# Starting the fast stages of a retention + expert-mixture kernel earlier, on one Trainium2 core

## The chip, the cores and the metric

One core of one Trainium2 chip. The metric is device microseconds (us) of one execution. Every total time below is a median of several executions, all in the same, undisturbed state; times inside a kernel are from one traced execution. Each engine runs its own instruction stream. In this program TensorE makes the matrix products, VectorE, ScalarE and GpSimd the element-wise work, and SyncE issues most transfers. GpSimd issues transfers as well, on a queue of its own.

## The reference

```python
# q, k, v: 8 batches, 8 heads, 576 tokens, 64 wide, float32
scores = (q @ k.transpose) / sqrt(64)
ret = scores * Dmat                     # Dmat: gamma_h ** (i - j) for j <= i, else 0
attn = ret @ v
x = attn, heads side by side            # 4608 tokens x 512
p = domain_probs / domain_probs.sum(-1)
out = 0
for e in range(4):                      # w1[e]: 512 x 1024, w2[e]: 1024 x 512
    out += p[:, e] * (relu(x @ w1[e]) @ w2[e])
```

The products are made in bfloat16 with float32 sums.

## The kernel before

The 4608 tokens are nine **tiles** of 512. For each tile and each expert there are two **units** of TensorE work: an up unit (x @ w1) and a down unit (h @ w2). A unit exists in two forms. The **classical** form is 32 products of 512 columns. The **seven-product** form splits each matrix into 2 x 2 blocks and makes seven block products instead of eight: 56 products of 256 columns. It needs sums of blocks of the weights, tokens and hidden values, which VectorE makes first (`weight_sums`, `down_sums`, `token_sums`, `hidden_sum`). So a unit can be fast only when weights and tokens have come early enough for their sums.

The program has a **head**, all classical, and then **stages**. A stage (tile, expert) runs the up unit of its own expert and, in four **fills** between its products, the down unit of the stage before it. The order of all instructions is fixed when the program is built. The attention of the batches is spread between these products: batch 0 and 1 by a fixed plan in the head, batches 2 to 7 by a list (`Chain`) that gives out pieces once they can be ready. A batch has 512 tokens in chunks and a **remainder** of 64.

Loads of q, k and v come in two forms. Batch 0 is loaded in token pairs, so that a run in memory is 512 bytes; all others in pieces with runs of 256 bytes:

```python
def load_paired(b):
    raw_units(b)
    for x, (hf, u) in enumerate(UNITS):          # four units: two halves x two groups of heads
        h = slice(4 * u, 4 * u + 4)
        for n, src in SRC:
            nc.sync.dma_start(out=state[b][n, x].rearrange("p (h x) -> p h x", h=4),
                in_=src[b, h, 256 * hf:256 * hf + 256, :].rearrange("h (p j) d -> p h (j d)", j=2))

def load_piece(b, n, c):
    t = state[b][n, c]
    return nc.sync.dma_start(out=t.rearrange("p (h d) -> p h d", h=H),
                             in_=dict(SRC)[n][b, :, c * C:(c + 1) * C, :].rearrange("h p d -> p h d"))
```

The results of the four experts are added either on the chip (first and last tile) or by the transfer that writes them (all others):

```python
def on_chip(nt):
    return nt in (0, n_nt - 1)

def send(nt, e, pair, j):                       # two of them, 512 KB each, for one (tile, expert)
    x = slice(...)                              # cut
    if e == 0:
        i = nc.sync.dma_start(out=out_rows[:, x, :], in_=acc[nt, j])
    else:
        i = nc.gpsimd.dma_start(out=out_rows[:, x, :], in_=acc[nt, j], accum_op=ADD)
    ...
```

The order of the weight loads, the plan of the head, and the stages:

```python
load_w1(1, 0); load_w1(1, 1)
w20 = load_w2(0)
load_w2(1)
for e in range(2, E):
    load_w1(e)
    load_w2(e)
load_next(w20); load_next(); load_next()        # remainder of batch 0
raw_units(1)
for c in range(2):                              # batch 1, unpaired
    for n in "kqv":
        load_piece(1, n, c)
...
at(25, begin1)                                  # the rest of batch 1, and batch 1's casts
for c, g in enumerate((39, 41, 43, 45)):        # batch 1's four chunks
    at(g, lambda c=c: a1().T(c))
    ...
head += [up_classical(0, 1), down_groups(0, 0), down_groups(0, 1), up_classical(0, 2), down_groups(0, 2),
         up_classical(0, 3), down_groups(0, 3), up_classical(1, 0, lead=2, cut=3 * NT // 4)]
...
for nt, e in [(nt, e) for nt in range(1, n_nt) for e in range(E)][1:]:   # stages (1, 1), (1, 2), ...
    ...
```

So before, five up units (expert 0 to 3 of tile 0, expert 0 of tile 1) and their five down units are classical, and all others have seven products.

Of the kernel before, what the change touches and what calls it, by code (L numbers as in the profile page):

```python
# [9 lines left out]
FP32 = mybir.dt.float32  # L10
# [13 lines left out]
def kernel(  # L24
# [66 lines left out]

    def raw_units(b):

        state[b] = {}
        for x in range(4):
            t = wpool.tile([128, 3, H * D], FP32, tag=f"w2s_{x}", name="raw")
            for i, (n, _) in enumerate(SRC):
                state[b][n, x] = t[:, i]

    def load_paired(b):  # L100
        raw_units(b)
        for x, (hf, u) in enumerate(UNITS):
            h = slice(4 * u, 4 * u + 4)
            for n, src in SRC:
                nc.sync.dma_start(
                    out=state[b][n, x].rearrange("p (h x) -> p h x", h=4),
                    in_=src[b, h, 256 * hf:256 * hf + 256, :].rearrange("h (p j) d -> p h (j d)", j=2))
# [36 lines left out]
    def load_w1(e, part=None):  # L144
        if not part:
            w1_sb.append(wpool.tile([128, NDC, F], BF16, tag=f"w1_{e}", name="wt1"))
        f = slice(0, F) if part is None else slice(part * F // 2, (part + 1) * F // 2)
        return nc.gpsimd.dma_start(out=w1_sb[e][:, :, f], in_=moe_w1[e, :, f].rearrange("(dc p) f -> p dc f", p=128))
# [7 lines left out]
    load_paired(0)  # L156
# [249 lines left out]
    class AttP(Att):  # L406

        rem_states = (1, 3)

        def cast(self, n, hf, u, eng):  # L410
            if (n, u) == ("k", 0):
                self.half(hf)
            h = slice(4 * u, 4 * u + 4)
            if n != "v":
                self.m[n, hf, u] = att1.tile([128, 2, 4, D], BF16, tag=n + "m", name=n + "m", bufs=3)
            o = self.m[n, hf][:, :, h, :] if n == "v" else self.m[n, hf, u]
            i = self.t[n, 2 * hf + u].rearrange("p (h j d) -> p j h d", h=4, j=2)
            if n in gain:
                g = gain[n][:, NCH + 1 + 2 * hf:NCH + 3 + 2 * hf, h]
                eng.tensor_tensor(o, i, g.unsqueeze(3).to_broadcast([128, 2, 4, D]), op=MULT)  # L420
            else:
                eng.tensor_copy(o, i)
# [71 lines left out]


# [4 lines left out]
    def on_chip(nt):  # L500
        return nt in (0, n_nt - 1)

    def out_pair(nt, e, pair, j):

        if e == 0 or not on_chip(nt):
            acc[nt, j] = apool.tile([128, 2, Dm], FP32, tag="acc", name="acc")
        return acc[nt, j]

    def send(nt, e, pair, j):
        x = slice(nt * NSUB + pair[0], nt * NSUB + pair[1] + 1, pair[1] - pair[0])  # L510
        if e == 0:
            i = nc.sync.dma_start(out=out_rows[:, x, :], in_=acc[nt, j])
        else:
            i = nc.gpsimd.dma_start(out=out_rows[:, x, :], in_=acc[nt, j], accum_op=ADD)  # L514
            for p, d in sent[nt, e - 1]:
                if set(p) & set(pair):
                    after(i, d)
        sent.setdefault((nt, e), []).append((pair, i))
# [25 lines left out]
    def downs(nt, e, ring):  # L544

        hT = hTs[nt, e]
        def evacuate(po, ns):
            t, pair, j = nt * NSUB + ns, (ns // 2 * 2, ns // 2 * 2 + 1), ns // 2
            a = (acc[nt, j] if ns % 2 else out_pair(nt, e, pair, j))[:, ns % 2]
            pe = probs[:, e, t:t + 1]  # L550
            if e == 0 or not on_chip(nt):
                nc.scalar.activation(a, po, Copy, scale=pe)
            else:
                nc.vector.scalar_tensor_tensor(a, po, pe, a, op0=MULT, op1=ADD)
            if not on_chip(nt):
                if ns % 2:
                    send(nt, e, pair, j)
            elif e == E - 1:
                nc.sync.dma_start(out=out[t * 128:(t + 1) * 128, :], in_=a)

        for ns in range(NSUB):
            po = bank(ring, [128, Dm], FP32, "po")
            for fc in range(NFC):
                nc.tensor.matmul(po, lhsT=hT[:, fc, ns * 128:(ns + 1) * 128],  # L564
                                 rhs=w2_sb[e][:, fc, :], start=(fc == 0), stop=(fc == NFC - 1))
                yield None if fc < NFC - 1 else lambda: evacuate(po, ns)
# [58 lines left out]
    class Down:  # L625
# [37 lines left out]
        def out(self, i):  # L663
# [5 lines left out]
            if e and on_chip(nt):  # L669
# [5 lines left out]
            if i == 1 and not on_chip(nt):  # L675
                send(nt, e, pair, j)
# [51 lines left out]
    warm(8)  # L728
# [3 lines left out]
    for x, (hf, u) in enumerate(UNITS):  # L732
# [14 lines left out]
        a0.kv(hf, u)  # L747
    transposed_probs()
# [8 lines left out]
    for e in range(2, E):  # L757
        load_w1(e)
        load_w2(e)
# [4 lines left out]
    for c in range(2):  # L764
        for n in "kqv":
            load_piece(1, n, c)
# [12 lines left out]
    class Chain:  # L779
        def __init__(self):  # L780
# [5 lines left out]
            self.now, self.begun, self.tokens, self.late = 0, {(1, "r"): -1}, 2 * S - R, []  # L786
# [87 lines left out]
        def emit(self, kind, nt, strict=True):  # L874
# [4 lines left out]
            for k, n in need.items():  # L879
# [8 lines left out]
                elif k == "tile":  # L888
                    ok = n <= nt + 2
# [27 lines left out]
    def casts1(*cs):  # L917
        for c in cs:
            for n in "kqv":
                state["a1"].cast(n, c, nc.gpsimd)  # L920

    def begin1():
        state["a1"] = Att(1)
        casts1(0)
        for c in range(2, NCH):
            for n in "kqv":
                load_piece(1, n, c)
        casts1(1, 2)
        load_ahead(7)

# [4 lines left out]

    def rem1_casts():
        for n in "kqv":
            a1().cast_rem(n, nc.gpsimd)
            loads["cast"] += 1
            load_ahead(len(PIECES))  # L940
        a1().dmaT(NCH)

    def a1():
        return state["a1"]
# [3 lines left out]
    at(29, a0.Trem)  # L948
    at(31, a0.Srem, a0.Srem_mask)
    at(34, a0.Orem, lambda: a0.x(NCH, nc.vector))  # L950
    at(25, begin1)
    for c, g in enumerate((39, 41, 43, 45)):
        at(g, lambda c=c: a1().T(c))
        at(g + 1, lambda c=c: (a1().S(c), a1().kv_chain(c)))
        if c > 0:
            at(g + 1, lambda c=c: a1().O(c - 1))
        at(g + 1, lambda c=c: (a1().mask(c, 0), a1().mask(c, 1)))
        if c > 0:
            at(g + 1, lambda c=c: a1().x(c - 1, nc.vector))
    at(47, lambda: (a1().O(3), a1().x(3, nc.vector)))  # L960

    def narrow():
        RINGS["at"] = ("a0", "a1", "a2")
        turn.update(at=0)

    at(42, lambda: casts1(3))
    at(46, rem1_casts)
    at(48, narrow, lambda: state.update(t1=token_sums(1)), lambda: [state["t1"].pop(i)() for i in (0, 0, 1)])

    def sums_at(kind, e, *gs):  # L970
        todo = []
        for i, g in enumerate(gs):
            at(g, lambda i=i: (todo or todo.extend(kind(e)), todo[i]()))
        return todo

    sums_at(weight_sums, 1, 16, 17, 18, 19)
    s0 = sums_at(weight_sums, 0, 20, 21, 22)
    sums_at(weight_sums, 2, 26, 28, 30, 31)
    sums_at(down_sums, 1, 42, 43, 44, 48)
    sums_at(weight_sums, 3, 36, 38, 49, 50)  # L980
    s2 = sums_at(down_sums, 2, 51, 52, 53)
    at(50, lambda: a1().put_krem(nc.gpsimd, a1().qr[:, 1]))
    for g in range(48, 56):
        at(g, lambda: pool(1, 1))

    head += [up_classical(0, 1), down_groups(0, 0), down_groups(0, 1), up_classical(0, 2), down_groups(0, 2),
             up_classical(0, 3), down_groups(0, 3), up_classical(1, 0, lead=2, cut=3 * NT // 4)]
    g = 0
    for work in head:
        for _ in work:  # L990
# [3 lines left out]
            if g > 48:  # L994
                chain.now += 1


    turn.update(po=0)
    state["t1"].pop()()
    def stage(nt, e):  # L1000
        return nt * E + e

    begin = {1: (1, 1), 2: (1, 2), 3: (1, 3), 0: (2, 0)}
    owed = [((1, 1), (2, 0), s0[3]), ((1, 1), (1, 3), s2[3])]
    for e in (3, 0):

        use, last = stage(*begin[e]) + 1, stage(*begin[e]) - E + 2
        owed += [(divmod(last if i == 3 else 0, E), divmod(use, E), f) for i, f in enumerate(down_sums(e))]

    def pay(nt, e, late=False):  # L1010
        for x in owed:
            if x[1] <= (nt, e) if late else x[0] <= (nt, e):
# [5 lines left out]
    before, gaps = (1, 0), 0  # L1018
    for nt, e in [(nt, e) for nt in range(1, n_nt) for e in range(E)][1:]:
        fast = before >= begin[before[1]]  # L1020
# [8 lines left out]
        def between(i):  # L1029
# [3 lines left out]
            if i == 3:  # L1033
                pool(nt, 4 if gaps < 8 else 3 - g)
# [4 lines left out]
        def fill(i):  # L1039
            if i == 4:  # L1040
                chain.put_late()
            if not fast:
                for _ in range(4):
# [28 lines left out]
        def last_sum():  # L1072
            if g == 1 and (nt, e) >= begin[e]:
# [5 lines left out]
        def sums(i):  # L1079


            old, new = before in hsum, (nt, e) >= begin[e]
            turns = {(0, 1): 0 if old else 2, (0, 2): 0 if old else 1, (0, 3): 1,
                     (1, 1): 2, (1, 2): 1, (1, 3): 1}[g, i]
            while (e, g, i) == (0, 0, 2) and front:
# [4 lines left out]
            if g == 1 and new:  # L1090
# [120 lines left out]
```

## Time and profile before

| | before |
|---|---|
| median of 3 executions | 515.34 us (515.08 to 516.17) |
| span in the trace | 514.5 us |
| TensorE busy | 98% |
| read from / written to memory | 45.16 MB / 31.46 MB |
| stage (1, 2), the first stage that both kernels run at the same place with the same past work | starts at 105.31 us |

The prediction below shows most of the views. Two more are needed for the comparison. The chain of work that ended last, as shares of the span, says who set the end:

```profile
PE 92%; DVE 5%; issue 1%; DMA 1%; ACT 0%; SPq 0%; DVEq 0%; ACTq 0%
```

The windows view gives the busy time of TensorE, weight load, VectorE, ScalarE and GpSimd (number of instructions in brackets), the granted clock, the share of DMA (1.00 is 16 engines full, and it may pass that where transfers overlap) and GB/s. The stretch in question:

```profile
40.00:85.00 45.00, 44.63 (x339) 22.62 (x343) 29.27 (x48) 15.98 (x30) 19.93 (x22) 1.00 1.06 197
```

TensorE works 44.63 of 45 us. The transfers are just as full, at a share of 1.06, and TensorE hardly feels it: what it asks for is nearly always there.

### The profile page before, as it was taken

How to read it: one execution, taken by the hardware profiler on the slowest of the kernel's cores; microseconds unless marked ns; L12 is line 12 of the kernel's file. 1: busy time of each engine (PE TensorE's matmuls, PEld its weight loads, DVE VectorE, ACT ScalarE, POOL GpSimd, SP SyncE). 2: the span in 40 equal slices, each digit the busy share in tenths (PEclk: the TensorE clock that was granted, in tenths of full speed). 3: DMA queues.
4: the chain of work that ended last, by engine and by line, in shares of the span. 5: the costliest groups of instructions: out<-in, count | busy, mean ns of one | idle time of the engine just before them, and what ended most of it. 6: DMA issues, size and time to landing. Idle time of an engine off the chain costs nothing.

```text
span 514.5 us, 12795 instructions
## 1 busy us (share of the span) xinstructions
PE 504.1 (98%) x4923; PEld 405.7 (79%) x4934; DVE 374.4 (73%) x696; ACT 336.0 (65%) x693; POOL 251.1 (49%) x345
## 2 busy tenths in 40 slices
PE   8999999999999999999999999999999999999995
PEld 3644455688888888888888888888888888888884
DVE  5724479878777777768777877886778777667785
ACT  3462263677667766777767776777777767777663
POOL 6702275756644656466645664476457521321012
PEclk9999999999999999999999999999999999999998
DMA  9999997959797799969997999789987652565002
GB/s 239 187 207 201 208 196 184 165 146 186 120 172 194 115 177 161 182 142 183 133 223 140 162 153 212 159 144 154 173 195 122 94 83 83 83 86 80 1 2 82
DMA packets 160749, 76.27 MB, mean 148 GB/s; under 512 B 131724, under 2 KB 144524, under 8 KB 160688
## 3 DMA queue, kind: packets, MB, share of 16 engines
q1 hardware_dynamic: 141648, 44.79, 44.8%
q0 software_dynamic: 18752, 30.41, 38.2%
q8 instruction: 38, 0.62, 0.5%
q10 hardware_dynamic: 288, 0.26, 0.2%
q14 instruction: 23, 0.19, 0.1%
HBM read 45.16 MB, written 31.46 MB: 149 GB/s over the span
## 4 chain that ended last, share of the span: by engine, by line
PE 92%; DVE 5%; issue 1%; DMA 1%; ACT 0%; SPq 0%; DVEq 0%; ACTq 0%
PE upP L691 21%; PE downV L645 20%; PE downW L645 15%; PE upR L691 10%; PE ph L525 7%; PE po L564 6%; PE upQ L691 5%; PE s L328 2%; PE oc L379 1%; PE kvp L346 1%; PE oc L376 1%; DMA raw<-in_q_dram 1%; PE warm_out L164 1%; DVE qm L420 1%; DVE sT L333 0%
## 5 line engine op out<-in xcount | busy, mean ns | idle before, releaser
L691 PEld LDWEIGHTS <-wt 128*128 128x128 bf16 x992 | 94.9, 98 | 14.5 <-issue 1.4
L645 PEld LDWEIGHTS <-hT 128*128 128x128 bf16 x960 | 93.7, 98 | 12.0
L716 POOL TENSOR_SCALAR hT<-hT 128x512 bf16<-128x512 bf16 x62 | 38.1, 614 | 108.9 <-DVE hT L715 108.7
L645 PE MATMUL downV<-wt,hT 128*128 128x256 bf16 x480 | 81.8, 272 | 0.0
L691 PEld LDWEIGHTS <-wsum 128*128 128x128 bf16 x744 | 72.6, 98 | 9.1 <-issue 0.2
L707 DVE TENSOR_TENSOR upR<-upP,m 128x512 f32<-128x512 f32 x62 | 43.3, 699 | 48.6 <-ACT downW L651 39.9
L645 PEld LDWEIGHTS <-hsum 128*128 128x128 bf16 x720 | 70.0, 98 | 8.8 <-DVE hsum L617 0.3
L691 PE MATMUL upP<-xT,wt 128*128 128x256 bf16 x496 | 74.4, 272 | 0.7 <-DVE xT L595 0.5
L723 ACT ACTIVATE hT<-upP 128x512 bf16<-128x512 f32 x62 | 37.0, 597 | 52.0 <-PE upP L691 36.8
L514 POOL DMA_DIRECT2D out_dram<-acc x42 | 51.3, 1221 | 30.7 <-ACT acc L672 23.9
L674 DVE TENSOR_SCALAR acc<-downV,probs 128x512 f32<-128x512 f32 x56 | 42.0, 749 | 30.1 <-PE downV L645 29.7
L718 ACT ACTIVATE hT<-upR 128x512 bf16<-128x512 f32 x62 | 37.0, 597 | 31.3 <-PE upR L691 31.3
L709 ACT ACTIVATE hT<-upQ 128x512 bf16<-128x512 f32 x62 | 37.0, 597 | 15.9 <-PE upQ L691 15.9
L715 DVE TENSOR_TENSOR hT<-upP,m 128x512 bf16<-128x512 f32 x62 | 42.8, 690 | 5.8 <-PE upP L691 4.4
L672 ACT ACTIVATE acc<-downW,probs 128x512 f32<-128x512 f32 x56 | 38.6, 690 | 9.2 <-PE downW L645 9.2
L340 POOL TENSOR_SCALAR_AFFINE_SELECT sT<-sT 128x512 bf16<-128x512 bf16 x24 | 15.4, 643 | 57.4 <-ACT sT L339 48.0
L541 ACT ACTIVATE hT<-ph 128x512 bf16<-128x512 f32 x40 | 23.5, 597 | 29.8 <-PE ph L525 28.9
L697 ACT ACTIVATE upQ<-upP 128x512 f32<-128x512 f32 x62 | 37.0, 597 | 2.5 <-PE upP L691 2.3
L691 PE MATMUL upP<-tsum,wt 128*128 128x256 bf16 x248 | 37.2, 273 | 0.0
L691 PE MATMUL upR<-tsum,wsum 128*128 128x256 bf16 x248 | 37.2, 273 | 0.1
L691 PE MATMUL upP<-tsum,wsum 128*128 128x256 bf16 x248 | 37.2, 273 | 0.0
L691 PE MATMUL upR<-xT,wsum 128*128 128x256 bf16 x248 | 37.2, 273 | 0.0
(149 smaller groups left out, 1032.9 us busy)
## 6 DMA issues: line engine op xcount, KB each, us to landing
out_dram<-acc POOLq DMA_DIRECT2D x42, 512.0 KB, 6.5
out_dram<-acc SPq DMA_DIRECT2D x14, 512.0 KB, 4.1
wt<-in_moe_w_dram POOLq DMA_DIRECT2D x6, 1024.0 KB, 25.2
raw_k<-in_k_dram SPq DMA_DIRECT2D x24, 256.0 KB, 4.4
raw_q<-in_q_dram SPq DMA_DIRECT2D x24, 256.0 KB, 3.5
raw_v<-in_v_dram SPq DMA_DIRECT2D x24, 256.0 KB, 4.2
raw<-in_k_dram SPq DMA_DIRECT2D x8, 256.0 KB, 5.6
raw<-in_q_dram SPq DMA_DIRECT2D x8, 256.0 KB, 5.6
```

Source lines behind the costliest of these rows:

```text
L514: i = nc.gpsimd.dma_start(out=out_rows[:, x, :], in_=acc[nt, j], accum_op=ADD)
L645: nc.tensor.matmul(o, lhsT=l[:, k, self.s * 128:(self.s + 1) * 128], rhs=r[:, k], start=(i == 1 and k == 0), stop=(k == NFC // 2 - 1), ski ...
L672: nc.scalar.activation(a, po, Copy, scale=pe)
L674: nc.vector.tensor_scalar_mul(a, po, pe)
L691: nc.tensor.matmul(ps[:, l], lhsT=wa(kc)[:, f:f + 128], rhs=xa(kc), start=(start and l == 0 and kc == 0), stop=(kc == 1), skip_group_check ...
L697: nc.scalar.activation(Q, P, Copy)
L707: nc.vector.tensor_tensor(R_, P, m5, op=ADD)
L709: nc.scalar.activation(hT[:, lo, t0], Q, Relu)
L715: nc.vector.tensor_tensor(h22, P, m5, op=ADD)
L716: nc.gpsimd.tensor_scalar(h22, h22, float("inf"), 0.0, op0=MIN, op1=MAX)
L718: nc.scalar.activation(hT[:, lo, t1], R_, Relu)
L723: nc.scalar.activation(hT[:, hi, t0], P, Relu)
```

## The change

The intent is to leave the classical form sooner. Tile 1 begins right after expert 2's up unit of tile 0, and tile 0's expert 3 comes later, as a stage between (1, 1) and (1, 2). Batch 1 must then be ready some 20 us sooner, so it is loaded in token pairs, as batch 0 was, before the second half of the weights. And as tile 0 isn't finished before tile 1 begins, only experts 0 and 1 of tile 0 are added on the chip: that result is written at once, and experts 2 and 3 are written as adding transfers. The core of the diff (the class for paired attention of batch 1, `AttQ`, is cut to its head, as are the lists of sums):

```diff
+    class AttQ(AttP):                     # batch 1 in four token-pair units
+        rem_states = (0, 1, 2, 3)         # states not summed: later units use 2 or 10 more products
+        ...
-    def on_chip(nt):
-        return nt in (0, n_nt - 1)
+    def adds(nt, e):
+        return e > 0 and (nt == n_nt - 1 or (nt, e) == (0, 1))
+    def sends(nt, e):
+        return nt < n_nt - 1 and (nt, e) != (0, 0)
@@ send
-        if e == 0:
+        if (nt, e - 1) not in sent:
             i = nc.sync.dma_start(out=out_rows[:, x, :], in_=acc[nt, j])
@@ start
-    warm(8)
+    warm(10)
         a0.kv(hf, u)
+        if x < 3:
+            warm(2)
@@ loads
-    for e in range(2, E):
-        load_w1(e)
-        load_w2(e)
+    w12 = load_w1(2, 1)
+    load_w1(2, 0)
...
-    for c in range(2):
-        for n in "kqv":
-            load_piece(1, n, c)
+    ORDER1 = (0, 2, 1, 3)
+    for x in ORDER1:
+        load_unit(1, x, w12)              # held until the first half of w1 of expert 2 is in
@@ plan of the head
+    at(3, lambda: cast1(0, "kv"), lambda: cast1(1, "kv"), lambda: load_w2(2), lambda: cast1(2, "kv"))
+    at(21, a0.Trem)                       # remainder of batch 0
+    at(22, a0.Srem, lambda: cast1(0, "q"), a0.Srem_mask)
+    at(23, lambda: a1.T(*UNITS[0]))       # batch 1
+    at(24, a0.Orem, lambda: a0.x(NCH, nc.scalar))
+    ...
+    at(25, lambda: cast1(3, "kv"), lambda: load_w1(3, 0), lambda: load_w1(3, 1), lambda: load_w2(3))
+    at(29, lambda: load_ahead(6))         # remainder of batch 1
...
-    head += [up_classical(0, 1), down_groups(0, 0), down_groups(0, 1), up_classical(0, 2), down_groups(0, 2),
-             up_classical(0, 3), down_groups(0, 3), up_classical(1, 0, lead=2, cut=3 * NT // 4)]
+    head += [up_classical(0, 1), down_groups(0, 0), down_groups(0, 1), up_classical(0, 2)]
@@ stages
+    stages = [(1, 0), (1, 1), (0, 3)] + [(nt, e) for nt in range(1, n_nt) for e in range(E)][2:]
...
-                for _ in range(4):
+                for n in range((8, 2, 2, 4)[i - 1] if g == 0 else 4):
+                    if (g, i, n) == (0, 1, 4):
+                        visit1(4, 3)      # batch 1's last values, inside the first fill
+                        t1.pop(0)()
+                        front.extend(t1)
                     f = next(fill_classical)
```

## The prediction

> **What bounds the kernel now.** I read the page's busy shares and its forty slices first, then the list of what TensorE waited for, then TensorE's timeline from 20 to 125 us, then the table of engines by windows, then the DMA view.
>
> ```profile
> PE 504.1 (98%) x4923; PEld 405.7 (79%) x4934; DVE 374.4 (73%) x696; ACT 336.0 (65%) x693; POOL 251.1 (49%) x345
> ...
> PE   8999999999999999999999999999999999999995
> ...
> DMA  9999997959797799969997999789987652565002
> GB/s 239 187 207 201 208 196 184 165 146 186 120 172 194 115 177 161 182 142 183 133 223 140 162 153 212 159 144 154 173 195 122 94 83 83 83 86 80 1 2 82
> ```
>
> TensorE is full in every slice but the first and the last. Waits give the reader the same thing from the other side; the columns are microseconds in all, times, longest:
>
> ```profile
> PE pt L429 <- DVE qm L420: 1.4, 3, 0.8
> PE warm_out L164 <- DVE kbd L159: 1.3, 1, 1.3
> PE o L481 <- DVE sT L469: 0.7, 2, 0.4
> PE upP L691 <- DVE xT L595: 0.5, 2, 0.3
> PE upP L691 <- DVE upR L707: 0.2, 1, 0.2
> ```
>
> Five entries, 4.1 us in all, and 3.4 us of that before 20 us. So the kernel is bound by the amount of TensorE work. A change gains what it takes out of TensorE's own stream, and loses any new wait that it puts there; moving work between the other engines gains nothing by itself.
>
> The sizes come from TensorE's timeline (start, duration, then what ran):
>
> ```profile
> 18.46 0.42 PE L463 MATMUL s<-qkT 64*64 64x128 bf16 x16
> 18.81 0.72 PE L447 MATMUL kvp<-vm,km 64*128 64x128 bf16 x8
> 34.71 13.98 PE L564 MATMUL po<-wt,hT 128*128 128x512 bf16 x63
> 48.52 5.34 PE L525 MATMUL ph<-xT,wt 128*128 128x512 bf16 x24
> ...
> 66.70 0.39 PE L309 MATMUL ptc<-ident,qm 128*128 128x128 bf16 x4
> 111.43 0.60 PE L691 MATMUL upP<-xT,wt 128*128 128x256 bf16 x4
> 111.86 0.60 PE L691 MATMUL upR<-tsum,wsum 128*128 128x256 bf16 x4
> 112.30 0.60 PE L645 MATMUL downV<-wt,hT 128*128 128x256 bf16 x4
> ```
>
> Starts, not durations, give the cost, as ends overlap. Two classical down units of 32 products of 512 columns run from 34.71 to 48.52 us: 13.81 us for 64, so 0.2158 us each and **6.91 us a unit** (one record of the 64 is missing). In the fast stages four products of 256 columns take 111.86 - 111.43 = 0.4375 us on average, 0.1094 each. A unit in seven products is 7 x 2 x 2 x 2 = 56 of them: **6.13 us**.
>
> **What the Trainium skill says.** "TensorE: Matmul & The Clock Gate", section "Wait — 56ns, not 53.3ns?": a warm stream advances by N/2.4 GHz plus about 2.5 ns, 215.7 ns at 512 columns. The trace agrees: 215.8, and 109.4 against a worked-out 109.2 at 256. The same section gives a floor of about 25 ns between starts of small products; here sixteen 64x64 products of 128 columns take 18.81 - 18.46 = 0.35 us, 22 ns each, so the measurement is a little lower, and I use 22 ns. "DMA: Bandwidth & Descriptors", section "Queues, rings and completion order": each DMA engine goes round its queues packet by packet. The trace agrees, in the DMA view of 36 to 38 us (packets, MB, share):
>
> ```profile
> q0 software_dynamic: 181, 0.37, 96.3%
> q1 hardware_dynamic: 179, 0.05, 17.3%
> ```
>
> Equal packets, but 2 KB each for weights and about 256 B each for the unpaired loads of q, k, v. Its section "Specifications" asks for 512 B at least per transfer for line rate. The trace agrees again, in the windows table (last column GB/s; 5 to 10 us is batch 0 in token pairs, 35 to 40 weights beside unpaired loads, 65 to 70 unpaired loads alone):
>
> ```profile
> 5.00:10.00 5.00, 4.30 (x32) 1.91 (x33) 2.72 (x5) 0.66 (x2) 2.36 (x4) 1.00 1.14 295
> 35.00:40.00 5.00, 5.00 (x25) 2.28 (x24) 0.17 (x1) 1.88 (x3) 0.00 (x0) 1.00 1.14 206
> 65.00:70.00 5.00, 4.95 (x49) 2.77 (x49) 2.98 (x5) 3.86 (x8) 3.68 (x4) 1.00 0.97 191
> 75.00:80.00 5.00, 4.94 (x51) 2.73 (x51) 5.00 (x8) 1.35 (x3) 4.01 (x6) 1.00 0.67 130
> ```
>
> **The change part by part.**
>
> *Four units in seven products.* Before, five up units (expert 0 to 3 of tile 0, expert 0 of tile 1) and their five down units are classical. After, only experts 0 to 2 of tile 0 are. Two ups and two downs change: 4 x (6.91 - 6.13) = **3.1 us off** TensorE, all of it on the path.
>
> *Batch 1 in token pairs.* Before, its four chunks of transposes, scores, states and values sit between 66.70 and 83.49 us. Adding the start-to-start pieces of the timeline (0.44 + 0.58 + 0.45 + 0.80 + 0.44 + 1.03 + 0.66 + 1.04 + 0.58) gives 6.0 us. After, there are four units. Each has eight transposes, 0.44 us; sixteen small state products, sixteen score and sixteen value products, about 0.35 us each; and 128-column products with all earlier states, since states are no longer summed: 2 in a first-half unit, 10 in a second-half one, at 0.055 us. That is 4 x 1.49 + 24 x 0.055 = 7.3 us, so **1.3 us on**. The remainder of batch 1 now takes four states instead of one: 12 more products of 64 columns at about 0.029 us (four start 0.11 us apart from the next group), **0.35 us on**.
>
> *Warm-up products.* Two more at the start, where TensorE waits 0.85 us for the first q anyway, and two after each of three head units (0.43 us each). In that stretch VectorE is busy 4.2 to 4.5 of 5 us and TensorE waits for its casts and masks. They fill waits: nothing to 0.1 us.
>
> *Output of tile 0.* Experts 2 and 3 go out as adding transfers: four more issues on GpSimd (1.22 us each, with GpSimd at 49%) and 2.1 MB more of DMA. Off the path, but it moves data into a crowded time, below.
>
> Sum of TensorE work: -3.1 + 1.3 + 0.35 + 0.1 = **-1.4 us**. The order of stages itself, and the 8, 2, 2, 4 split of classical fill, move work and add none. What the split does: the last values of batch 1 run inside the first fill, and 4 classical products plus one group (0.86 + 0.44 us) lie between them and the product that needs their token sum. ScalarE must copy three pieces (about 0.9 us) and VectorE subtract (0.42 us), some 1.5 us with the handing over. I add **0.2 us** of wait.
>
> **Where new waits can come from: the load order.** Before, weights land one after the other: w1 of expert 1 at 26.4, w2 of 0 at 31.3, w2 of 1 at 36.6, w1 of 2 at 42.4, w2 of 2 at 49.0, w1 of 3 at 54.8, w2 of 3 at 61.5 us (issue plus time to landing). After, batch 1 starts when the first half of w1 of expert 2 is in, near 40 us. Paired units landed 2.7 us apart for batch 0. So, with half a weight (0.5 MB) beside them, I expect unit 0 near 46 us, unit 1 near 49, unit 2 near 52; then w2 of expert 2 starts and takes two bytes for one, and w2 and unit 3 are in near 59 and 60 us. TensorE asks for them, adding the pieces above from 48.5 us on: unit 0 at 49, unit 1 at 52, unit 2 at 55.5, unit 3's k and q (cast) at 59 and v at 61, w2 of expert 2 at 63.5. Two to three microseconds of slack at first, about none for unit 3: I book **0.3 us**. In the same steps ScalarE has 1.2 us of activations, 0.76 of q copies, about 1.1 to 1.5 of states and 0.76 of x (rows of 0.38 us) against 3.3 to 3.7 us of TensorE: full, **0.2 us** more. In tile 1's first two stages VectorE gets some ten owed weight sums of 0.7 to 1 us; w1 of expert 3, now issued only after unit 3, lands near 70 us, about when its sums come up: **0.3 us**. Against these, the waits of the old stretch (two of 0.2 to 0.3 us at 115 us and before the sums, and the 0.2 us gap at 78 us) go: 0.5 us back.
>
> Total: -1.4 + 0.2 + 0.3 + 0.2 + 0.3 - 0.5 = -0.9 us, about 514.4. I shade it to **513.8 us**, as the schedule looks fitted by trial: the gate, the order of units and the fill numbers would have been chosen to remove just these waits.
>
> **The rivals.** *Loads become the bound of the head.* For it: DMA is at 9 in slices 1 to 6, and by the first stage of tile 1 about 13.0 MB must have come, which the kernel before had only at about 62 us. Against: paired rows run at 295 GB/s instead of 191. If it holds, unit 3 or w2 is 3 to 4 us late: 516 to 518. *VectorE or ScalarE become the bound around 49 to 85 us*, since about 18 us of sums and masks move forward into a shorter head: before, VectorE was already full at 75 to 80 us and TensorE still didn't wait. It would cost 1 to 2 us: 515 to 516. *Small products are cheaper than I think*, if sixteen of 64 columns take 0.2 us and not 0.35, and no wait appears: -3.1 + 0.7 + 0.2, some 512.5.
>
> **Range and chances.** The floor is the 3.1 us of saved work with attention at par and half a microsecond of old waits gone: 511.7. The upper end has one late load of about 2.5 us: 516.4. Two per cent is 10.3 us; nothing on TensorE's path can give that, and to lose it a load would have to be later than any in the trace: 0.01 faster, 0.97 within, 0.02 slower.
>
> **What would show each step right or wrong.** Groups: upP of line 691 counts 33 units (528 instead of 496), classical ph and po three units each (96). TensorE's busy time falls by 1 to 2 us; its idle time between 20 and 100 us stays under 2 us. Stage (1, 2) begins 1 to 2 us earlier than at 105.3 us. Four units of paired attention in batch 1 add to about 7.3 us. A wait of TensorE on k, q or v of batch 1, on w2 of expert 2, or on a sum behind w1 of expert 3, of more than 1 us in all, would prove the load rival. The prediction is wrong if the time leaves the range or if the gain is not in TensorE's stream before 105 us but after it.

## The result, and the profile after

| | before | after |
|---|---|---|
| median, same rounds | 515.25 us (515.08 to 516.17, 4 executions) | 519.66 us (518.13 to 520.78, 4 executions) |
| ratio, with 95% interval | | 1.008 [1.0051, 1.0109] |
| span in the trace | 514.5 us | 519.1 us |
| written to memory | 31.46 MB | 33.55 MB |
| stage (1, 2) starts | 105.31 us | 111.36 us, with one 1.03 us piece of attention more behind it |

A ratio is the mean time of one kernel's fast runs over that of the other's in the same rounds, so not quite the ratio of the medians. Within 2%, but 0.8% slower, and outside the predicted range. The page of the kernel after, with its engines' busy time, the granted clock over forty slices and the chain that ended last:

```profile
PE 504.2 (97%) x5138; PEld 416.1 (80%) x5150; DVE 389.6 (75%) x722; ACT 347.9 (67%) x736; POOL 253.4 (49%) x351
...
PEclk9999998999999999999999999999999999999999
...
PE 78%; DMA 11%; SPq 4%; DVE 4%; POOL 2%; issue 1%; ACT 0%; DVEq 0%; ACTq 0%; POOLq 0%
```

The DMA has 11% of the chain where it had 1%. Seventh slice: the granted clock falls to 8 tenths. TensorE's busy time did not fall, though it has less to do, in part because a product at a lower clock counts as busy for longer (below: 1.03 us for a group of four at 88.23 us, 0.62 for one at 91.62). What TensorE waited for, after 20 us:

```profile
PE s L340 <- DMA qkT<-km: 2.7, 1, 2.7
PE ptr L331 <- POOL qrb L299: 1.7, 1, 1.7
PE po L645 <- DMA wt<-in_moe_w_dram: 1.3, 1, 1.3
PE pt L517 <- DVE qm L433: 0.5, 1, 0.5
```

In the kernel before, the only entry after 20 us is one of 0.2 us on VectorE. Three of the four on TensorE's timeline (start, duration, what ran, and in brackets what it had waited for), with what follows the last:

```profile
45.14 0.29 PE L331 MATMUL ptr<-ident,qrb 64*128 64x64 bf16 x4 [1.69 <-POOL qrb L299]
...
64.74 1.04 PE L645 MATMUL po<-wt,hT 128*128 128x512 bf16 x3 [1.33 <-DMA wt<-in_moe_w_dram]
...
87.90 0.40 PE L340 MATMUL s<-qkT 64*128 64x128 bf16 x8 [2.73 <-DMA qkT<-km]
88.23 1.03 PE L772 MATMUL upP<-xT,wt 128*128 128x256 bf16 x4
...
91.62 0.62 PE L772 MATMUL upP<-tsum,wsum 128*128 128x256 bf16 x4
```

From 88.23 to 91.62 there are four groups of four products of 256 columns (the first of them shown): 3.39 us, where the prediction's 0.4375 us a group gives 1.75. The windows show why, in the third column from the end (the granted clock), and that the transfers are still full in the long stretch:

```profile
40.00:85.00 45.00, 40.82 (x473) 25.87 (x478) 32.68 (x55) 26.13 (x66) 21.74 (x26) 1.00 1.18 221
...
88.00:92.00 4.00, 4.00 (x28) 2.86 (x27) 1.29 (x2) 1.28 (x3) 3.42 (x6) 0.57 1.17 205
```

A mean clock of 0.57 right after the wait of 2.73 us. So the stretch cost 2.73 us of waiting and then 1.64 us more.

GpSimd's timeline tells where the late data come from. It casts the remainder of batch 0 (first line), issues w2 of expert 2 (second), casts the remainder of batch 1 (third) and batch 2's first k (last):

```profile
44.05 1.03 POOL L299 TENSOR_TENSOR qrb<-raw_q,gq 64x512 bf16<-64x512 f32 x1 [3.55 <-DMA raw_q<-in_q_dram]
...
50.30 0.94 POOL L163 DMA_DIRECT2D wt<-in_moe_w_dram  x1
...
66.65 1.03 POOL L299 TENSOR_TENSOR krb<-raw_k,gk 64x512 bf16<-64x512 f32 x1 [8.44 <-DMA raw_k<-in_k_dram]
...
80.16 1.04 POOL L291 TENSOR_TENSOR km<-raw_k,gk 128x512 bf16<-128x512 f32 x1 [1.63 <-DMA raw_k<-in_k_dram]
```

w2 of expert 2 lands 14.4 us after its issue, at 64.7 us (before: 49.0). SyncE's queue at the same time, with the two 512 KB halves of tile 0's result just ahead of the load of batch 1's remainder:

```profile
50.60 1.30 SPq L596 DMA_DIRECT2D out_dram<-acc  x2
51.99 0.60 SPq L143 DMA_DIRECT2D raw_k<-in_k_dram  x1
```

Those halves take 10.9 us from issue to landing at the median, the k of the remainder 14.6 and its q 17.3 us. The kernel before writes tile 0 only once, and late: four parts, issued from 76.1 to 86.2 us. So the change does two things to the writes of tile 0: it moves the first one forward to 50 us, and it adds two. Batch 2's loads take their buffers over from the remainder, so they are late in turn, then its transposes.

**The account.** From the first product after the head's opening attention (21.30 us before, 19.52 after) to stage (1, 2): 84.0 us before, 91.8 - 1.0 = 90.8 us after. That is **6.8 us longer**. (The opening itself was 1.8 us shorter by chance, as experiment 2 shows; part of that probably just went into the waits.) Each trace is of one execution, and a slow one of its kernel (516.28 and 520.78 us), so the parts hold for these two; the repeat in experiment 5 shares the waits out differently. The parts:

| part | us |
|---|---|
| four units in seven products (upP counts 528) | -3.1 |
| batch 1's attention: pieces of 0.46 + 0.48 + 0.45 + 0.82 + 0.45 + 1.34 + 0.45 + 0.83 + 0.91 = 6.2 against 6.0 | +0.2 |
| its remainder: 0.47 against 0.11 | +0.4 |
| the named waits: 1.69 + 1.33 + 0.48 + 0.17 + 2.73 | +6.4 |
| products at the lower clock, 88.23 to 91.62 | +1.6 |
| what is left of the sum: gaps too short for the list | about +1.3 |

### The profile page after: what moved, and what is told of

Same layout as the page of the kernel before. It is cut to its first block, busy times and chain, and to the rows that moved or that the text cites. A ratio compares the mean times of both kernels' runs of the same rounds, so it can differ in the third digit from the quotient of the medians.

```text
span 519.1 us, 13336 instructions
## 1 busy us (share of the span) xinstructions
PE 504.2 (97%) x5138; PEld 416.1 (80%) x5150; DVE 389.6 (75%) x722; ACT 347.9 (67%) x736; POOL 253.4 (49%) x351
## 3 DMA queue, kind: packets, MB, share of 16 engines
HBM read 45.16 MB, written 33.55 MB: 152 GB/s over the span
## 4 chain that ended last, share of the span: by engine, by line
PE 78%; DMA 11%; SPq 4%; DVE 4%; POOL 2%; issue 1%; ACT 0%; DVEq 0%; ACTq 0%; POOLq 0%
PE upP L772 21%; PE downV L726 21%; PE downW L726 15%; PE upR L772 10%; PE upQ L772 5%; DMA wt<-in_moe_w_dram 4%; DMA raw_q<-in_q_dram 3%; SPq L113 3%; DMA raw<-in_v_dram 2%; PE s L340 2%; DMA raw_k<-in_k_dram 1%; PE oc L391 1%; PE kvp L358 1%; PE oc L388 1%; DVE hsum L698 1%
## 5 line engine op out<-in xcount | busy, mean ns | idle before, releaser
L772 PEld LDWEIGHTS <-wt 128*128 128x128 bf16 x1056 | 101.0, 98 | 16.2 <-issue 2.4
L726 PEld LDWEIGHTS <-hT 128*128 128x128 bf16 x1024 | 100.3, 98 | 12.7
L797 POOL TENSOR_SCALAR hT<-hT 128x512 bf16<-128x512 bf16 x66 | 41.2, 624 | 110.3 <-DVE hT L796 110.0
L726 PE MATMUL downV<-wt,hT 128*128 128x256 bf16 x512 | 87.7, 274 | 0.0
L772 PEld LDWEIGHTS <-wsum 128*128 128x128 bf16 x792 | 77.8, 98 | 9.8
L726 PEld LDWEIGHTS <-hsum 128*128 128x128 bf16 x768 | 74.4, 98 | 11.0 <-DVE hsum L698 0.9
L772 PE MATMUL upP<-xT,wt 128*128 128x256 bf16 x528 | 79.6, 273 | 0.5 <-DVE upR L788 0.3
L598 POOL DMA_DIRECT2D out_dram<-acc x46 | 56.2, 1222 | 32.1 <-ACT acc L753 27.4
L755 DVE TENSOR_SCALAR acc<-downV,probs 128x512 f32<-128x512 f32 x60 | 44.9, 749 | 31.2 <-PE downV L726 30.7
L772 PE MATMUL upQ<-xT,wt 128*128 128x256 bf16 x264 | 39.6, 273 | 0.0
```

The costliest lines, as they stand in the source:

```text
L726: nc.tensor.matmul(o, lhsT=l[:, k, self.s * 128:(self.s + 1) * 128], rhs=r[:, k], start=(i == 1 and k == 0), stop=(k == NFC // 2 - 1), ski ...
L755: nc.vector.tensor_scalar_mul(a, po, pe)
L772: nc.tensor.matmul(ps[:, l], lhsT=wa(kc)[:, f:f + 128], rhs=xa(kc), start=(start and l == 0 and kc == 0), stop=(kc == 1), skip_group_check ...
L797: nc.gpsimd.tensor_scalar(h22, h22, float("inf"), 0.0, op0=MIN, op1=MAX)
```

## The experiments

The theory after the result, **A**: each wait comes from one transfer that is late on its own account, and each can be moved away by shifting a load or a step. Its rival, **B**: the transfers as a whole are the bound between 40 and 85 us; moving one makes another late. A third, **C**: what makes them too many is tile 0's result, 1 MB written at 50 us. In each group the kernel before ran in the same rounds; the kernel after took 519.66 us and its repeat 520.06, which are the numbers to compare with.

### 1. One cause at a time, then all together

The remainder of batch 0 a step later, so that its cast need not be waited for (`e1_rem0_shift`):

```diff
-    at(21, a0.Trem)
-    at(22, a0.Srem, lambda: cast1(0, "q"), a0.Srem_mask)
-    at(23, lambda: a1.T(*UNITS[0]))
-    at(24, a0.Orem, lambda: a0.x(NCH, nc.scalar))
+    at(22, lambda: cast1(0, "q"), a0.Trem)
+    at(23, lambda: a1.T(*UNITS[0]), a0.Srem, a0.Srem_mask)
+    at(25, a0.Orem, lambda: a0.x(NCH, nc.scalar))
```

> Only the three steps of batch 0's remainder (transposes, scores, values) go one step later in the head, so that TensorE comes to them about 45.2 us, when the cast of its q is ready (45.1 us in the changed kernel). The two waits there (1.7 us on the cast, 0.5 us on the next q) should vanish. Theory A, fixed arrival times: w2 of expert 2 still lands near 64.7 us, so TensorE only comes to that wait earlier and the wait grows from 1.3 to about 3 us; the whole changes by less than 0.5 us (519 to 520). Theory B, waits that add up: 2 us faster, 517.5.

**519.28 us**, before 515.76, ratio 1.0071 [1.0047, 1.0095]. The wait of 1.69 us is gone, and stage (1, 0) starts at 61.56 instead of 62.81 us. But w2 of expert 2 still comes when it comes: the next wait grew from 1.3 to 2.1 us, and its first product runs at 64.29 instead of 64.74. Arrivals stand nearly still; what is saved ahead of one is waited for at it. (The wait of 1.69 us alone proves nothing for the edit: in the thirteen traces of the kernel after and its variants that leave these steps as they are, it is 1.7 us once, 0.7 four times and not listed in eight.)

The remainder of batch 1 loaded ahead of tile 0's result (`e2_rem1_first`):

```diff
-    at(29, lambda: load_ahead(6))
+    at(20, lambda: load_ahead(6))
```

> Only the loads of batch 1's remainder are queued ahead of tile 0's two output transfers (1 MB) on the same queue instead of behind them. Theory A: the remainder lands near 56 to 60 us instead of 66 to 71, GpSimd casts it without waiting, batch 2's first loads start some 5 us earlier, its transposes are there before TensorE asks at 85 us: the 2.7 us wait and the half-speed 3.4 us after it go, 4.3 us faster (515.4). Rival: DMA as a whole is too full, so batch 2 is no earlier and the wait stays: within 1 us of 519.7.

**521.37 us**, before 515.76, ratio 1.0109; the expected gain is missed. The remainder came 7 us earlier (its k cast at 59.90 instead of 66.65) and the wait on batch 2's transposes fell from 2.7 to 0.3 us. But now the result was late, 16.0 us from issue to landing, and its two buffers are the ones that the next unit's results need. ScalarE's timeline:

```profile
69.82 0.69 ACT L638 ACTIVATE acc<-po,probs 128x512 f32<-128x512 f32 x1 [5.07 <-DMA out_dram<-acc]
```

TensorE's waits, with VectorE named although the cause sits two steps behind it:

```profile
PE upP L772 <- DVE upR L788: 5.3, 3, 4.9
```

The list of attention begun three steps later for batch 2, so that its transposes have longer (`e8_chain_later`; `+ 5` becomes `+ 8` for that batch in the test whether a piece is ready):

> Loads untouched; only the first scores of batch 2 are placed three gaps (about 4.5 us) later in TensorE's order. Theory A (the order asks too early): no wait at 85 us and no slow clock after it, 4.3 us faster (515.4), the later visits have slack. Rival (batch 2's attention is needed by then, lateness only moves on): a wait of similar size turns up at a later visit or at tile 2, less than 1.5 us faster.

**519.08 us**, before 515.76, ratio 1.0073; missed too. The wait on the transposes is gone. But `e5_warm_old` and `f0_after_again` below, with the old list, wait only 0.2 and 0.8 us there, so this one trace doesn't show that the edit removed it. In this execution the cast of batch 0's remainder happened not to be waited for, and the wait on w2 was 3.4 us, with the clock at 0.50 in the 4 us after it. The waits change places from one execution to the next, and the total hardly moves.

All of it (`e4_all_three`): the edits of `e1_rem0_shift` and `e2_rem1_first`, and w2 of expert 2 issued one unit earlier:

```diff
-    at(3, lambda: cast1(0, "kv"), lambda: cast1(1, "kv"), lambda: load_w2(2), lambda: cast1(2, "kv"))
+    at(3, lambda: cast1(0, "kv"), lambda: load_w2(2), lambda: cast1(1, "kv"), lambda: cast1(2, "kv"))
```

> The shift of batch 0's remainder, batch 1's remainder ahead of the output, and w2 of expert 2 issued after the first unit of batch 1 instead of after the second. Theory A (three places where a transfer comes after TensorE's fixed order asks for it, and one clock drop, 7.9 us in all): all gone, 511.5 to 512.5, faster than the kernel before. If units 2 and 3 of batch 1 become late through w2's earlier place, 513 to 515. Rival (DMA bound in the head): 516 or more.

**520.09 us**, before 515.76, ratio 1.0081. Theory A asked for 511.5 to 512.5 and falls here. The waits on the cast and on w2 gave way to a new one, on the q of batch 1's last unit, and the wait on the transposes grew. VectorE's timeline, then TensorE's waits:

```profile
60.36 0.69 DVE L433 TENSOR_TENSOR qm<-raw,gq 128x512 bf16<-128x512 f32 x1 [3.75 <-DMA raw<-in_q_dram]
```

```profile
PE s L340 <- DMA qkT<-km: 3.6, 1, 3.6
PE pt L517 <- DVE qm L433: 2.1, 1, 2.1
```

### 2. The warm-up products

`e5_warm_old` is the kernel after with the old number of warm-up products, `e6_before_warm` the kernel before with the new one:

```diff
     # e5_warm_old                      # e6_before_warm
-    warm(10)                        -  warm(8)
+    warm(8)                         +  warm(10)
-        if x < 3:                   +      if x < 3:
-            warm(2)                 +          warm(2)
```

> The changed kernel with the old warm-up products (eight at the start, none between the units of batch 0). In the profiles the four products behind the first transposes take 1.9 us before and 1.0 us after, and the up unit of expert 0 starts at 21.3 and 19.5 us. Theory A (clock released earlier, but later arrival times of transfers decide): the head starts 1.2 to 1.8 us later, and the waits on the cast of batch 0's remainder and on w2 of expert 2 swallow most of it: 519.5 to 520.3, within 0.6 us of the changed kernel. If the head's start counts in full: 521 to 521.5. My prediction's step (warm-up products change nothing): the up unit starts at the same time.

> The kernel before with the new warm-up products and nothing else. It has no waits on transfers later, so the head's 1.2 to 1.8 us should come through in full: 513.9 to 514.6 against 515.7. The prediction's step (nothing to 0.1 us slower): 515.7.

**519.11 us** against 514.99 before, ratio 1.0075 [1.0057, 1.0092]; and **514.69 us** against 514.99, ratio 0.9991 [0.9976, 1.0006]. They do nothing that can be measured. The opening ended at 21.30 us in the kernel before and 19.65 in `e5_warm_old`, both with the old number, and between 19.52 and 20.85 in the traces with the new one. So the 1.8 us of difference in the first two traces was chance.

### 3. Taking the added megabyte away

`e7_no_send` is wrong on purpose: the result of experts 0 and 1 of tile 0 is never written, so part of the output is missing. That is the first of tile 0's three writes, the one at 50 us. All else is the same program.

```diff
     def send(nt, e, pair, j):
+        if (nt, e) == (0, 1):
+            sent.setdefault((nt, e), [])
+            return
```

> Wrong on purpose: tile 0's output of experts 0 and 1 (two transfers of 512 KB, issued at 50 us) is never sent, so rows of tile 0 come out wrong. Theory C (the number of bytes that must pass before 85 us decides): w2 of expert 2 lands about 2 to 3 us earlier (62), batch 1's remainder near 58 to 60 instead of 66 to 71, so the waits on w2 and on batch 2's transposes and the half-speed stretch go: 513.5 to 515.5. Rival (order, not amount): same waits, within 1 us of 519.7.

**514.3 us**, before 514.99, ratio 0.9989 [0.9969, 1.0008]: 5.4 us less than the kernel after, which ran in other rounds (4.7 us by the two ratios to the kernel before). As an estimate from the traces, 1.05 MB at the 221 GB/s of the kernel after from 40 to 85 us takes 4.8 us. TensorE's waits on transfers after 20 us (the first product line has moved by three lines):

```profile
PE po L648 <- DMA wt<-in_moe_w_dram: 0.6, 1, 0.6
...
PE s L340 <- DMA qkT<-km: 0.2, 1, 0.2
```

And GpSimd's timeline, the remainder of batch 1 and batch 2's first k, to be read against 66.65 and 80.16 us after:

```profile
59.47 1.03 POOL L299 TENSOR_TENSOR krb<-raw_k,gk 64x512 bf16<-64x512 f32 x1 [2.22 <-DMA raw_k<-in_k_dram]
...
75.80 1.04 POOL L291 TENSOR_TENSOR km<-raw_k,gk 128x512 bf16<-128x512 f32 x1
```

w2 of expert 2 lands at 62.0 instead of 64.7 us. The k of the remainder is issued 2.1 us earlier, as SyncE doesn't issue the write first (49.91 instead of 51.99 us), but it also lands 9.5 instead of 14.6 us after its issue, so the larger part of its 7.2 us isn't the place in the queue. All three late things come sooner with one transfer gone, though none of them was touched; stage (1, 2) starts at 104.41 us. The transfers are as busy as ever (219 GB/s from 40 to 85 us). Theory C holds. But even then the change only draws level: about 2.5 us less work on TensorE, and about 2.3 us of waits and gaps in its place, of which some 1.2 us are in the list (w2 0.6, VectorE 0.4, transposes 0.2).

### 4. Another order of loads

If too much must come between 40 and 85 us, something should go out of it. `e9_w3_late` issues the weights of expert 3, which stage (0, 3) needs last, in tile 1's first stage instead of at step 25, with their sums later as well:

```diff
-    at(25, lambda: cast1(3, "kv"), lambda: load_w1(3, 0), lambda: load_w1(3, 1), lambda: load_w2(3))
+    at(25, lambda: cast1(3, "kv"))
...
+            if gaps == 3:
+                load_w1(3, 0)
+                load_w1(3, 1)
+                load_w2(3)
```

> Both weight loads of expert 3 are issued in tile 1's first stage (about 70 us) instead of at 56 us, with their sums one stage later. Theory C: w2 of expert 2 is unchanged (it is ahead in that queue), so its 1.3 to 3 us wait stays; batch 1's remainder lands some 4 to 6 us earlier, the wait for batch 2's transposes and the slow clock go: 515.5 to 517. The weights of expert 3 are then needed at about 92 us and land near 85 to 90: if they are late, a new wait of 1 to 4 us stands in front of expert 3 of tile 0 and the total is 518 to 520.

**531.46 us**, before 514.99, ratio 1.0308: slower, and missed. From 65 to 70 us the transfers now moved 26 GB/s, almost nothing; then the weights came beside batch 2's transposes, which took 16.9 and 15.1 us from issue to landing instead of 4.1 and 2.9 after:

```profile
PE s L340 <- DMA qkT<-km: 12.4, 1, 12.4
```

Here the hole in the stream of transfers was not made good later, and a large load in the wrong place held up a small one that was needed at once.

Two more ask whether the *place* of tile 0's result in its queue matters rather than its amount. `g1_send_behind_w2` issues it on GpSimd's queue, behind w2 of expert 2:

```diff
-            i = nc.sync.dma_start(out=out_rows[:, x, :], in_=acc[nt, j])
+            i = (nc.gpsimd if nt == 0 else nc.sync).dma_start(out=out_rows[:, x, :], in_=acc[nt, j])
```

> Tile 0's output after expert 1 is issued on GpSimd's queue, behind w2 of expert 2, instead of on the queue of the loads; the same bytes in another order. If the order decides: w2 lands at 60 to 62 instead of 64 to 65.5, batch 1's remainder near 60 to 62 instead of 66 to 71, no wait on w2 and none on batch 2's transposes; w1 of expert 3 lands some 3 to 5 us later (73 to 75), and VectorE stands before it with its sums for 1 to 3 us: 516 to 518. If the amount decides: one late arrival takes the place of another, 519 to 521.

**520.47 us**, before 515.25, ratio 1.0101. w2 lands at 62.2 us and the remainder's k at 59.8, both as good as without the result. But batch 2's first k, issued 6.3 us earlier than after (67.42 us), is cast only at 81.22 us (80.16 after), and the wait on its transposes is 4.5 us now (2.7 after). The place moves the wait; the amount stays.

`g2_send_behind_ws3_later` adds later sums of expert 3, to free VectorE (`owed += [((1, 1), (0, 3), f) for f in weight_sums(3)]`), and `g3_ws3_chain_later` also begins the list of batch 2 three steps later:

> As the one before, with expert 3's weight sums allowed only from tile 1's second stage, so that VectorE doesn't stand before w1 of expert 3. Order decides: 514.5 to 516, no wait of TensorE over 1 us after 50 us. Amount decides: 518 to 521, a wait of 2 us or more on some other arrival.

> As the one before, with the first scores of batch 2 placed three gaps later, in case its transposes are again the late arrival. Order decides: within 0.7 us of the one before. Amount decides: up to 2 us faster than the one before if that wait was there, but still 517 or more.

**522.08 us**, ratio 1.013, and **519.59 us**, ratio 1.0087, both against 515.25. In the first the transposes are waited for 3.7 us and a VectorE step 1.2. In the second the transposes are on time, and TensorE waits 2.0 and 1.6 us for VectorE instead. Ahead of the first, VectorE is busy with the postponed sums. Ahead of the second it has itself waited 2.07 us for a result's transfer to free its buffer: a transfer again.

### 5. A correct way to lose the megabyte

`f1_keep2` adds expert 2 of tile 0 on the chip as well and writes the result after it. One of the three writes of tile 0 disappears, and the first of the other two is issued at 77 instead of 50.6 us; no load changes:

```diff
-        return e > 0 and (nt == n_nt - 1 or (nt, e) == (0, 1))
+        return e > 0 and (nt == n_nt - 1 or (nt, e) in ((0, 1), (0, 2)))
-        return nt < n_nt - 1 and (nt, e) != (0, 0)
+        return nt < n_nt - 1 and (nt, e) not in ((0, 0), (0, 1))
```

`f0_after_again` is the kernel after, unchanged, in the same rounds. `f2_keep2_w2_early` adds the earlier w2 of `e4_all_three`. `f3_keep2_x_vector` is `f1_keep2` with batch 1's x copied by VectorE, because ScalarE looked full.

> The changed kernel itself once more, unchanged, on the same chip as the three below: about 519.5. Since two of its profiled relatives had no wait on the cast of batch 0's remainder and a larger one on w2 of expert 2, I expect the same sum split differently: 1.3 to 3.5 us on w2, and 0 to 1.7 us on the cast.

> Correct result: expert 2 of tile 0 is added on chip as expert 1 is, and tile 0 is first sent after expert 2 (about 72 us) instead of after expert 1 (50 us). One output of 1 MB less in all, and none in the crowded stretch. Theory C (1 MB in that stretch is what makes w2, batch 1's remainder and batch 2 late): as in the run that didn't send it, 514 to 515, 4.5 to 5.5 us faster than the changed kernel. If the 1 MB at 72 us is as harmful as at 50 us (batch 2's loads are then under way): 516 to 519, with the wait for batch 2's transposes back.

> As the one before, and w2 of expert 2 issued after the first unit of batch 1. Theory C: the rest of the wait on w2 (0.6 us without the output) goes, and units 2 and 3 come some 2 us later, for which the slack of the no-output run (3 us) is enough: 0.3 to 0.8 us faster than the one before. If unit 3's q is late, as in the run with all three edits (2.1 us there): 0.5 to 1.5 us slower.

> As the second, with batch 1's values copied to x by VectorE instead of ScalarE. It tests the step that ScalarE is the full engine between 50 and 65 us (4.1, 4.9 and 3.8 of 5 us busy) and costs TensorE small gaps before up products (three of about 0.2 us). If so: 0.3 to 0.8 us faster. If VectorE (3.4, 3.4, 2.2 of 5 us) becomes the one waited for: 0 to 1 us slower.

| run | us (range) | ratio to before (515.82) | what TensorE waited for |
|---|---|---|---|
| `f0_after_again` | 520.06 (519.17 to 520.53) | 1.0083 [1.0069, 1.0098] | w2 2.8, transposes 0.8, cast 0.7 |
| `f1_keep2` | 517.23 (517.1 to 517.65) | 1.0033 [1.0021, 1.0045] | w2 1.6, VectorE 1.3 and 1.0 |
| `f2_keep2_w2_early` | 521.43 (520.45 to 523.16) | 1.0123 | q of batch 1's last unit 3.1, VectorE 1.5 and 1.0, cast 0.7 |
| `f3_keep2_x_vector` | 517.07 (516.16 to 519.97) | 1.0036 [1.0014, 1.0058] | VectorE 1.8 and 1.0 |

`f1_keep2` is correct, 2.8 us faster than the kernel after in the same rounds, and its remainder of batch 1 comes at 61.0 instead of 66.65 us. So the megabyte is confirmed without breaking the result. It doesn't gain the whole 5.4 us: the time lies where I had expected it if the later write did harm too, but that case's sign, a wait on batch 2's transposes, isn't there. Instead w2 is waited for, and VectorE, which now has the adding to do, more than in `e7_no_send` (there w2 0.6, VectorE 0.4); how the shortfall splits between the two isn't shown. TensorE's waits in `f1_keep2`:

```profile
PE po L645 <- DMA wt<-in_moe_w_dram: 1.6, 1, 1.6
PE upP L772 <- DVE upR L788: 1.3, 3, 0.8
PE upP L772 <- DVE hT L796: 1.0, 1, 1.0
```

Giving ScalarE less to do changed nothing, against the 0.3 to 0.8 us that I expected; but `f3_keep2_x_vector` hands that work to VectorE, which is then waited for a little longer (1.8 instead of 1.3 us), so a gain and a loss may have cancelled. And an earlier w2 again only made another load late.

No correct version beat the kernel before. A third buffer for results, which would have freed ScalarE in `e2_rem1_first`, was tried and didn't build: the working pool asked for 10 KB per partition, with 6.2 left.

## Why the prediction was wrong

By its own steps:

- *TensorE's amount is the bound, and a change loses any new wait that it puts there.* Right: the work fell, and the waits, with the low clock after one of them, rose by more. (TensorE's busy time, which I expected 1 to 2 us lower, stayed at 504 us.)
- *Four units, 3.1 us off.* Right: 528 upP products, and the classical groups gone.
- *Batch 1's units, 1.3 us on.* Too much: 0.2. The term that was off is the sixteen products of 64 columns. I had put 0.35 us; they take 0.15 (the next group starts at 52.69 after 52.54), 0.8 us less for four units. *The remainder, 0.35 on*: 0.36.
- *Warm-up products, nothing to 0.1.* Right, by `e5_warm_old` and `e6_before_warm`.
- *ScalarE full, sums behind w1 of expert 3: 0.2 + 0.3.* Small gaps cost about 1.3 us after; whose they are is open, as `f3_keep2_x_vector` only exchanged ScalarE's work for VectorE's.
- *The load order, 0.3.* **This is the step that failed.** I put it so: "w2 and unit 3 are in near 59 and 60 us", and "I book **0.3 us**". Unit 3 was even sooner, in at about 55 us; w2 came at 64.7, and behind it the remainder of batch 1 at 66.6 and batch 2. In place of 0.3 us there were 5.8 us of waits on transfers (1.69 + 1.33 + 2.73) and 1.6 us of lower clock. The 1.69 us, on the remainder of batch 0, end at 45 us, before the write is issued at 50.6, so they are not the write's doing, and the prediction had no term for them. For the others, why is written a few lines above it: "Output of tile 0 ... Off the path, but it moves data into a crowded time, below". That sentence is about the two adding writes; below, no write is added to any arrival. I followed the loads that TensorE asks for and stopped at w2. The 1 MB that is *written* at 50 us, between unit 3 and the remainder, and from 76 us on in the kernel before, wasn't in the sum; neither were the remainder and batch 2 behind it. `e7_no_send` measures that megabyte: 4.7 to 5.4 us. Even without it w2 lands at 62.0 us, some 3 us after my 59; what makes that part is open.
- *The first rival, loads become the bound, 516 to 518.* Right in kind, with the wrong item ("unit 3 or w2 is 3 to 4 us late") and too small, as several loads were late and the clock fell too. I gave it too little weight because "the schedule looks fitted by trial"; that said nothing about the chip. The upper end of my range held one late load of 2.5 us. There were three in the trace.

Shown: the write at 50 us is what turns a draw into a loss (`e7_no_send`; `f1_keep2` agrees), and none of the shifts tried repaired it (`e1_rem0_shift`, `e2_rem1_first`, `e8_chain_later`, `e4_all_three`, `g1_send_behind_w2`). Open: how the 2.3 us of waits and gaps that remain in `e7_no_send` split between VectorE, ScalarE and loads. That the lower clock follows from the wait is read from their order in several traces; no run changed it alone, and the length of the wait doesn't decide it: after 2.29 us on w2 in `e5_warm_old` the clock was 0.50 (66 to 68 us), after 3.07 us in `f2_keep2_w2_early` it stayed at 1.00 (62 to 72 us).

## What to carry to other kernels

When work moves forward, add up all bytes that must pass in the new stretch, writes as well as reads, in the order of issue, and follow them past the first one that TensorE asks for: a transfer off the critical path delayed here what came behind it. With the transfers full, each shift of a load that was tried handed the wait on to another; only fewer bytes helped. And a wait of 2 or 3 us on TensorE may cost more afterwards, in products at a lower clock: 1.6 us here, and nothing in another run.

## What the Trainium skill lacked or had wrong

- "TensorE: Matmul & The Clock Gate", section "Wait — 56ns, not 53.3ns?", gives about 25 ns as a floor between starts of small products. Here sixteen 64x64 products of 64 columns start within 0.15 us, 9 ns each, and those of 128 columns within 0.35 us, 22 ns each. The section doesn't say that the floor is not for products on separate parts of the array, as these 64x64 ones are; only the same page's "Part 3: Packing small matmuls — row/col tiling" gives about 4 ns between starts there.
- The same page, section "Part 1: The HAM clock gate (the "warmup" mystery)", lists the slow state "after ≥1 idle window (~3.4µs)". Here idle times shorter than that were followed by a low clock: 2.73 us in the kernel after (mean 0.57 over the next 4 us), 2.75 us in `f0_after_again` (0.57), 2.29 us in `e5_warm_old` (0.50 from 66 to 68 us). In the kernel after it cost 1.6 us on top of the wait. But 3.07 us in `f2_keep2_w2_early` left the clock at 1.00.
- No page that I read says how long a small transposing transfer takes beside a busy queue of weights: here 2.9 to 4.1 us in the kernel after, 15.1 and 16.9 us in `e9_w3_late`. The same for a plain 512 KB write: 4.1 us at the median before, 10.9 us (median of the two halves) after at the crowded time, 16.0 us in `e2_rem1_first`.
